# Cosine attention and a Fourier mixing layer on one core: a new order of all steps up to the first product

## The chip, the core and the metric

The kernel runs on one core of a Trainium2 chip. The metric is the device time of one execution in microseconds (us). The core's engines are TensorE (PE, with its weight loads as PEld), VectorE (DVE), ScalarE (ACT), GpSimd (POOL) and SyncE (SP); SP and POOL issue the loads, each on a DMA queue of its own.

## What is computed

Eight batches of 12 heads with 448 tokens and 64 columns. Attention works with q and k of length one; its result, 448 tokens by 768 columns, goes through a two-dimensional Fourier transform, of which the real part is added to it; then come layer normalization and a feed-forward block with 3072 hidden units and a ReLU:

```python
q_n = q / (np.linalg.norm(q, axis=-1, keepdims=True) + 1e-06)
k_n = k / (np.linalg.norm(k, axis=-1, keepdims=True) + 1e-06)
scores = np.matmul(q_n, k_n.transpose(0, 1, 3, 2)) / tau
scores = scores - np.max(scores, axis=-1, keepdims=True)
attn = np.exp(scores)
attn = attn / (np.sum(attn, axis=-1, keepdims=True) + 1e-09)
attn_out = np.matmul(attn, v)
x = attn_out.transpose(0, 2, 1, 3).reshape(B, S, H * D)
u = x + np.real(np.fft.fft(np.fft.fft(x, axis=1), axis=2))
un = (u - mean(u)) / np.sqrt(var(u) + 1e-06)
out = u + np.maximum(un @ w_ch1, 0.0) @ w_ch2
```

## The kernel before

**Stages.** The batches follow each other, and each overlaps with its neighbours: while TensorE works on the feed-forward products of batch b, the other engines prepare the heads of batch b + 1, and the attention products of b + 1 go in between. Only batch 0 has nothing ahead of it. Its start is a chain: loads of q, k and v; norms; scalings; transposes; scores; exponentials; products with v; the Fourier transform; layer normalization; and then the first product with w_ch1. The change touches this start above all.

**Names of the start, with their lines.** The twelve heads lie in six pairs, loaded in three groups: pair 0, pairs 1 and 2, pairs 3 to 5. A group has three tiles: K and Q with 384 columns for each pair (tokens 0 to 383), and a tail T with 128 columns for each pair (the last 64 tokens of q and of k). `first_norm` makes for each group:
- `ld_k`, `ld_q`, `ld_t`: the loads, on SP's queue (L1139). Before any run the planner has a list, QUEUES, with the order of the first loads of both queues; the change leaves it as it is. The v loads (L1315 to L1318), then the loads of w_ch1 (`W1_0` to `W1_11`, L1066) and of w_ch2 are on GpSimd's queue.
- `sqK`, `sqQ`, `sqT` (ACT, L1146): squares of a tile; `ssK`, `ssQ`, `ssT` (DVE, L1149): their sums for each token and head.
- `ln` (ACT, L1085), `nrm` (ACT, L1087, the root as an exponential of half the logarithm), `eps` (DVE, L1088), `rcp` (DVE, L1089): the reciprocal of norm plus epsilon.
- `scK`, `scQ` (L1172) and `scT` (L1168): the scalings of a pair, on DVE or on POOL, whichever the plan finds better.
- `tk`, `tq`, `tt` (PE, L1195 to L1220): transposes; `ek`, `eq` (L1186) and `et` (L1230, into the block-diagonal KTD) take them out of PSUM. KTD is cleared once by POOL (`ktd0`, L1009).

Then for each pair: scores `qk` (PE, L1360 and L1373), four exponentials `ex` (ACT, L1338, each over two PSUM banks of 450 columns), products with v `pv` (PE, L1391, L1397), the sums' reciprocal `rd` (L1415) and the division `x` (L1417). `fold` adds and subtracts mirrored tokens (L1434, L1441, L1468, a copy of eight columns L2101), since the transform is worked out on sums and differences. `fs` (PE, L1525) is the transform over the columns, `te` (L1547, ACT or DVE) takes it out of PSUM, `fd` (PE, L1568) is the transform over the tokens, and `u` (DVE, L1632) adds it to x with the sums for the mean. Layer normalization: `ba` (DVE, L1658, the mean), `bs` (ACT, L1662, the variance pass over 768 columns), `un` (DVE, L1674, the centred halves), `tn` (PE, L1683, transposes), `eu` (L1691, evacuations into UNT). A first product `h` is L1758: w_ch1 by UNT, first with one tile of 128 tokens (`h` of row tile 0 alone), later with a pair of row tiles (256 columns). A ReLU (L1774) follows, then the products with w_ch2 (L1902) and the output additions `fin` (POOL L1928, DVE L1939). The Fourier tables are made in the start too: sines and cosines (ACT, L1032, L1034), a negated copy of one table (`sinp` POOL L1046, `sinn` DVE L1052), halves of two rows (`half`, ACT L1049), and three loads of ScalarE's function tables (L1040, L1042, L1053). POOL makes index tables with small iotas (`ix`, L1018).

While batch 0 goes through its layer normalization, the norms of batch 1 begin in the same code (`sqK0_1`, `ssK0_1` and so on), on the same engines.

**What sets the order.** Nothing is written in the order in which it runs. Each step is an operation with its engines, its durations, a priority, the operations that it depends on (`deps`: these become semaphore waits in the program) and operations that it only has to come behind in the plan (`order`: no wait). `Plan.schedule` (L644) then simulates all engines in the builder, and at each point takes for an engine, among the operations that could start first, the one of lowest priority number. Its result is a fixed sequence for each engine. Each engine's instructions run in just that sequence, whatever the real times are. Three tables move the result: SHIFT adds a number to the priority of one operation; FLOW says how long a load takes; and LATE is a margin by which the plan puts an operation later than its load's planned landing, so that the real engine doesn't stand in front of it:

```python
            op.prio = round(op.prio + SHIFT.get(op.name, {}).get(k, 0), 4)
```

## Time and profile before

| | before |
|---|---|
| time, median of 3 runs | 575.67 us (575.16 to 577.59) |
| the profiled execution's own time | 574.34 us |
| its span in the trace | 572.5 us |
| granted TensorE clock, share of full speed | 1.0 |
| TensorE matmul busy | 552.2 us (96%), 6598 instructions |
| TensorE weight loads busy (beside the matmuls) | 432.6 us (76%) |
| VectorE busy | 439.6 us (77%), 926 instructions |
| ScalarE busy | 382.8 us (67%), 723 instructions |
| GpSimd busy | 231.5 us (40%), 338 instructions |

The rows say how long each engine worked within the span; they overlap, so they don't add up to it. The span is the traced part of the profiled execution, 1.84 us shorter than the execution's own time; that time is 1.33 us below the median of the runs. Cut into forty slices of 14.3 us each, TensorE is busy for 3 tenths of the first slice, 7 of the second, nine or more of the third and all that follow, and 8 of the last. The chain of work that ended last lies for 75% of the span on TensorE, 17% on VectorE and 5% on ScalarE.

### The profile page before, as it was taken

How to read it: one execution, taken by the hardware profiler on the slowest of the kernel's cores; microseconds unless marked ns; L12 is line 12 of the kernel's file. 1: busy time of each engine (PE TensorE's matmuls, PEld its weight loads, DVE VectorE, ACT ScalarE, POOL GpSimd, SP SyncE). 2: the span in 40 equal slices, each digit the busy share in tenths (PEclk: the TensorE clock that was granted, in tenths of full speed). 3: DMA queues.
4: the chain of work that ended last, by engine and by line, in shares of the span. 5: the costliest groups of instructions: out<-in, count | busy, mean ns of one | idle time of the engine just before them, and what ended most of it. 6: DMA issues, size and time to landing. Idle time of an engine off the chain costs nothing.

```text
span 572.5 us, 15993 instructions
## 1 busy us (share of the span) xinstructions
PE 552.2 (96%) x6598; PEld 432.6 (76%) x6598; DVE 439.6 (77%) x926; ACT 382.8 (67%) x723; POOL 231.5 (40%) x338
## 2 busy tenths in 40 slices
PE   3799999999999999999999999999999999999998
PEld 3569787686787678868778787687786886969695
DVE  8989857988488768886879668977986497987363
ACT  7898895565876676798458775696456752747171
POOL 8534424347345535453471536344532103031303
PEclk9999999999999999999999999999999999999999
DMA  9999998985349938953695549553933100023001
GB/s 193 210 239 174 170 181 123 161 180 109 113 68 114 171 87 126 138 125 92 121 125 109 83 109 132 116 128 54 142 65 34 62 1 26 32 41 73 21 36 56
DMA packets 187897, 62.19 MB, mean 109 GB/s; under 512 B 166800, under 2 KB 185616, under 8 KB 187824
## 3 DMA queue, kind: packets, MB, share of 16 engines
q1 hardware_dynamic: 129856, 38.35, 36.2%
q0 software_dynamic: 57968, 22.81, 36.0%
q8 instruction: 52, 0.85, 0.6%
q14 instruction: 21, 0.17, 0.1%
HBM read 51.90 MB, written 11.01 MB: 110 GB/s over the span
## 4 chain that ended last, share of the span: by engine, by line
PE 75%; DVE 17%; ACT 5%; issue 2%; POOL 1%; DMA 0%; DVEq 0%; POOLq 0%; ACTq 0%
PE PS L1902 26%; PE PS L1758 26%; PE PS L1853 6%; PE PS L1397 6%; PE PS L1360 5%; DVE U L1620 3%; DVE HQ L2002 2%; PE PS L1391 2%; ACT E L1338 2%; PE PS L1373 1%; DVE ACG L1609 1%; PE PS L1525 1%; DVE U L1632 1%; DVE OUTB L1939 1%; DVE SM L1272 1%
## 5 line engine op out<-in xcount | busy, mean ns | idle before, releaser
L1758 PE MATMUL PS<-UNT,W1b 128*128 128x256 bf16 (+1 forms) x1728 | 185.3, 264 | 1.2 <-ACT KTD L1230 0.4
L1758 PEld LDWEIGHTS PS<-UNT,W1b 128*128 128x128 bf16 x1728 | 154.0, 98 | 21.3 <-issue 1.7
L1338 ACT ACTIVATE E<-PS 128x900 bf16<-128x900 f32 (+1 forms) x192 | 149.3, 827 | 28.6 <-PE PS L1360 24.6
L1902 PE MATMUL PS<-W2b,HQ 128*128 128x384 bf16 x720 | 124.8, 326 | 0.0
L1283 POOL TENSOR_TENSOR QH<-STG,SM 128x256 bf16<-128x256 f32 x126 | 87.4, 720 | 90.9 <-DVE SM L1089 64.7
L1928 POOL TENSOR_TENSOR OUTB<-OUTB,U 128x192 f32<-128x192 f32 x72 | 50.8, 725 | 127.0 <-ACT OUTB L1923 125.8
L1902 PEld LDWEIGHTS PS<-W2b,HQ 128*128 128x128 bf16 x720 | 68.8, 98 | 43.3 <-issue 0.6
L1902 PE MATMUL PS<-TX,HQ 128*128 128x384 bf16 (+2 forms) x444 | 76.7, 322 | 1.6 <-DVE OUTB L1939 1.4
L1774 ACT ACTIVATE HQ<-PS 128x512 bf16<-128x512 f32 x82 | 48.8, 597 | 37.9 <-PE PS L1758 37.0
L1902 PEld LDWEIGHTS PS<-TX,HQ 128*128 128x128 bf16 x444 | 41.4, 98 | 28.2 <-DVE OUTB L1939 2.5
L2002 DVE TENSOR_TENSOR HQ<-HQ 128x1536 bf16<-128x1536 bf16 (+1 forms) x73 | 55.1, 758 | 9.1 <-ACT HQ L1774 6.3
L1272 DVE TENSOR_REDUCE SM<-QH 128x6 f32<-128x384 f32 x84 | 45.1, 544 | 13.1 <-ACT QH L1270 12.5
L1397 PE MATMUL PS<-VB,E 128*128 128x65 bf16 x1152 | 51.9, 193 | 0.0
L1270 ACT ACTIVATE QH<-STG 128x384 f32<-128x384 f32 x84 | 43.0, 521 | 10.3 <-DVE SM L1272 9.5
L1397 PEld LDWEIGHTS PS<-VB,E 128*128 128x128 bf16 x1152 | 47.9, 97 | 1.5
L1961 POOL DMA_INDIRECT out_dram<-OUTB,IDX x21 | 23.4, 1115 | 57.5 <-DVE OUTB L1939 30.1
L1774 DVE TENSOR_SCALAR HQ<-PS 128x512 bf16<-128x512 f32 x44 | 30.1, 684 | 19.7 <-PE PS L1758 19.1
L1391 PE MATMUL PS<-VZ,E 128*128 128x130 bf16 x192 | 41.6, 219 | 1.0 <-ACT E L1338 0.9
L1662 ACT ACTIVATE F<-U,MV 128x768 bf16<-128x768 bf16 x28 | 26.2, 934 | 21.2 <-DVE MV L1657 17.8
L1620 DVE SCALAR_TENSOR_TENSOR U<-ACG,X 128x768 bf16<-128x768 f32 (+4 forms) x39 | 39.3, 1014 | 0.7
L1360 PE MATMUL PS<-QK 64*128 64x225 bf16 (+2 forms) x864 | 39.1, 227 | 0.1
L1923 ACT ACTIVATE OUTB<-PS 128x384 f32<-128x384 f32 x36 | 17.6, 488 | 29.5 <-PE PS L1902 29.2
(193 smaller groups left out, 784.3 us busy)
## 6 DMA issues: line engine op xcount, KB each, us to landing
STG<-in_k_dram SPq DMA_DIRECT2D x18, 384.0 KB, 4.6
STG<-in_q_dram SPq DMA_DIRECT2D x18, 384.0 KB, 3.7
VB<-in_v_dram POOLq DMA_DIRECT2D x24, 192.0 KB, 6.7
W1b<-in_moe_w_ch_dram POOLq DMA_DIRECT2D x12, 384.0 KB, 8.0
W2b<-in_moe_w_ch_dram POOLq DMA_DIRECT2D x12, 384.0 KB, 6.7
out_dram<-OUTB SPq DMA_DIRECT2D x7, 384.0 KB, 4.4
W2b<-in_q_dram SPq DMA_DIRECT2D x2, 576.0 KB, 10.1
W2b<-in_k_dram SPq DMA_DIRECT2D x2, 576.0 KB, 11.0
```

What stands on the lines that cost most here:

```text
L1272: P.add("dve", lambda v, o=SS[:, i, H // ns * x:H // ns * (x + 1)], sq=sq: v.tensor_reduce(o, sq.rearrange("p (h d) -> p h d", d=DH), AX.X ...
L1283: r = v.tensor_tensor(v3(qh)[:, h:h + 4], v3(buf)[:, h:h + 4], RN[:, i, h:h + 4].unsqueeze(2).to_broadcast((128, 4, DH)), AluOp.mult)
L1338: return a.activation(o, self.PS[:, bk:bk + nc_, 0:SQ2], ACTF.Exp, scale=1.0 / self.tau)
L1360: i = pe.matmul(self.PS[:, bk + h, c0:c0 + n], self.KT[r, jj, kt * 128:(kt + 1) * 128], self.QT[r, jj, cols], start=True, stop=True)
L1391: r = pe.matmul(o, st(6), self.VZ[:, j, :], start=not split, stop=(split and i == 0), skip_group_check=True)
L1397: r = pe.matmul(o[:, 65 * h:65 * h + 65], st(2 * kt + h), self.VB[:, kt, 2 * j + h, :], start=(split and i == h == kt == 0), stop=((not sp ...
L1620: self.snu.append(P.add("dve", lambda v: v.scalar_tensor_tensor(two(U[o0:o0 + n, ut, :]), src, 1.0, two(X[i0:i0 + n, x, :]), AluOp.mult, A ...
L1758: r = pe.matmul(self.PS[:, bk, x * n:(x + 1) * n], self.W1b[:, j, ft * 128:(ft + 1) * 128], self.UNT[:, j, cs], start=(j == 0), stop=(j == ...
L1774: return e.activation(o, i, ACTF.Relu) if e is self.nc.scalar else e.tensor_relu(o, i)
L1902: r = pe.matmul(self.PS[:, bk, 0:n], lhs(f), rhs(f), start=(start and f == 0), stop=(stop and f == NF // 2 - 1), skip_group_check=True)
L1928: r = g.tensor_tensor(self.OUTB[:, ob, xs], self.OUTB[:, ob, xs], self.U[:, ut, xs], AluOp.add)
L2002: P.add("dve", lambda v: v.tensor_tensor(cs(o), cs(a), cs(bq), op), 0.16 + 0.3 * len(ks), -0.5, f"{nm}{ks[0]}_{b}", reads=rd, writes=[x fo ...
```

## The change

Five things are changed; the instructions themselves stay what they were, but for the engine that some of them run on.

1. **The table SHIFT is replaced as a whole**, up to the last batch. So the sequence of every engine is another one, in the start and behind it.
2. **Margins.** LATE gets six entries for the start: for the squares of the second group's K (0.85) and T (0.95), of the third group's Q (1.25), T (2.6) and K (2.3), and for the first product with v (2.6). In the plan these now come that much behind the planned landings.
3. **The clearing of KTD** (`ktd0`) gets a real dependency on the first scalings of pair 0, K, Q and T. So it waits for VectorE in the program, where it waited for nothing of that kind.
4. **The scalings of pair 0** can run on VectorE only; the plan had put one on GpSimd.
5. **Orders for the plan** (no waits): GpSimd's small iotas (`ix`) and the clearing of pads come behind the last v load of batch 0; the transform's second half `fd` of batch 0 is chained; the squares of K and T of batch 1 come behind ScalarE's `te`; their sums come behind the first two `eu`; the variance pass `bs` of the first row tile comes behind its `eu`; the residual additions from the third on behind its `un`; the copies `cd1` to `cd5` (the mirrored half of a table) behind its `eu`; and the last function table load behind `te`.

```diff
 SHIFT = {
...
-    "scK0_0": {0: 40.2716}, "scQ0_0": {0: 379.426}, "scT0_0": {0: 381.7288}, "et0_0": {0: 8.4556}, "ld_k1_0": {0: 119.799},
...
-LATE = {r"sq6_[2-7]": 4.0, r"W[12]_\d+": 1.5, "tmd": 2.0, r"sq\d_\d": 2.0, r"sq[KQT]\d_1": 1.5, ...
+LATE = {r"sqK1_0": 0.85, r"sqT1_0": 0.95, r"sqQ2_0": 1.25, r"sqT2_0": 2.6, r"sqK2_0": 2.3, r"pv00_0": 2.6, r"sq6_[2-7]": 4.0, ...
...
-        P.add("pool", lambda g: g.memset(self.KTD[:], 0.0), 0.8, -3, "ktd0", after=[tas],
+        self.ktd0 = P.add("pool", lambda g: g.memset(self.KTD[:], 0.0), 0.8, -3, "ktd0", after=[tas],
...
                 P.add("act", lambda e, sq=sq, buf=buf: e.activation(sq, buf, ACTF.Square), t_act(w), pg[g], f"sq{nm}{g}_{b}",
-                      reads=names, writes=sqn[g][i], order=[self.exps[-1]] if b else [])
+                      reads=names, writes=sqn[g][i], order=[self.exps[-1]] + self.te[1:] * (i != 1) if b else [])
...
-                                 t_dve(w), pg[g], f"ss{nm}{g}_{b}", reads=sqn[g][i], writes=[f"SS_{a + j}{i}" for j in range(n)], order=sc if b else []))
+                                 t_dve(w), pg[g], f"ss{nm}{g}_{b}", reads=sqn[g][i], writes=[f"SS_{a + j}{i}" for j in range(n)], order=sc + self.un0 * (i != 1) if b else []))
...
-                    sc.append(P.add("dve" if b else ("dve", "pool"), fn, ...
+                    sc.append(P.add(("dve", "pool") if b == 0 and g else "dve", fn, ...
                                     writes=qhn[g][i] if j == 0 else [qhn[g][i][-1] + f"_{j}"],
                                     after=[sc0[i]] if j else []))
                     if j == 0:
                         sc0.append(sc[-1])
+                        if (b, g) == (0, 0):
+                            self.ktd0.deps.add(sc[-1])
...
             self.vl.append(op)
+            if b == 0 and t == 3:
+                for x in P.ops:
+                    if re.fullmatch(r"ix\d+|pads", x.name):
+                        x.order = tuple(x.order) + (op,)
...
-            P.add(es, ev, [t_act(n_) if e == "act" else t_dve(n_) for e in es], pj, f"te{blk}_{b}",
+            te = P.add(es, ev, [t_act(n_) if e == "act" else t_dve(n_) for e in es], pj, f"te{blk}_{b}",
...
+            if es == ("act",):
+                self.te.append(te)
...
-                                         tiles=(tile,), acquire=tile if sg or b else None, margin=0.2))
+                                         tiles=(tile,), acquire=tile if sg or b else None, margin=0.2, order=self.fd_ops[-1:] if b == 0 else ()))
...
-            P.add("act", lambda a, ut=ut, ns_=ns_, mean=mean, var=var: a.activation(
+            bs = P.add("act", lambda a, ut=ut, ns_=ns_, mean=mean, var=var: a.activation(
...
+                if late:
+                    bs.order = tuple(bs.order) + tuple(P.ops[-2:])
+                    self.un0 = P.ops[-2:]
+                    for u in [x for x in self.snu[2:] if x.name == "u0_0"] + [x for x in self.snu if x.name == "u1_0"]:
+                        u.order = tuple(u.order) + (un,)
+                    for x in P.ops:
+                        if x.name in ("cd1", "cd2", "cd3", "cd4", "cd5"):
+                            x.order = tuple(x.order) + tuple(self.un0)
+                    self.ldt.order = tuple(self.ldt.order) + tuple(self.te)
```

The three places below show the sequence of one engine each. Line numbers are those of the two kernels apart: in the changed kernel the same line stands some 55 higher (L1146 is now L1201, L1172 is L1227, L1066 is L1121).

ScalarE near its start, before: squares (into HQ and W2b), the two halved rows (CS, 1x225), a table load, the logarithm (L1085) and root (L1087) of pair 0's norms, the squares of the second group's T, K and Q, the first evacuation (into QK).

```order
L1146 ACTIVATE HQ<-TX 128x384
L1049 ACTIVATE CS<-CS 1x225
L1146 ACTIVATE HQ<-TX 128x128
L1049 ACTIVATE CS<-CS 1x225
L1040 ACT_TABLE_LOAD
L1085 ACTIVATE SM<-SM,MV 128x14
L1087 ACTIVATE SM<-SM 128x14
L1146 ACTIVATE HQ<-TX 128x256
L1146 ACTIVATE W2b<-TX 128x768
L1146 ACTIVATE HQ<-TX 128x1152
L1186 ACTIVATE QK<-PS 128x384
```

The same place after:

```order
L1201 ACTIVATE HQ<-TX 128x128
L1201 ACTIVATE HQ<-TX 128x384
L1095 ACT_TABLE_LOAD
L1140 ACTIVATE SM<-SM,MV 128x14
L1104 ACTIVATE CS<-CS 1x225
L1142 ACTIVATE SM<-SM 128x14
L1104 ACTIVATE CS<-CS 1x225
L1201 ACTIVATE HQ<-TX 128x1152
L1201 ACTIVATE HQ<-TX 128x256
L1201 ACTIVATE W2b<-TX 128x768
L1243 ACTIVATE QK<-PS 128x384
```

The two halved rows come behind the logarithm, one of them between it and the root, and the wide square of Q (128x1152) comes ahead of the squares of T and K.

GpSimd behind its v loads and index tables, before: loads of w_ch1 with scalings of T (TX) and of K and Q (QH) among them.

```order
L1066 DMA W1b<-in_moe_w_ch_dram 128x6x256 x2
L1168 TENSOR_TENSOR TX<-TX,SM 128x128
L1066 DMA W1b<-in_moe_w_ch_dram 128x6x256
L1172 TENSOR_TENSOR QH<-TX,SM 128x384
L1066 DMA W1b<-in_moe_w_ch_dram 128x6x256
L1168 TENSOR_TENSOR TX<-TX,SM 128x128
L1172 TENSOR_TENSOR QH<-TX,SM 128x384
L1066 DMA W1b<-in_moe_w_ch_dram 128x6x256
L1172 TENSOR_TENSOR QH<-TX,SM 128x384
L1066 DMA W1b<-in_moe_w_ch_dram 128x6x256 x4
```

The same place after:

```order
L1064 MEMSET KTD 128x768
L1121 DMA W1b<-in_moe_w_ch_dram 128x6x256 x3
L1223 TENSOR_TENSOR TX<-TX,SM 128x128
L1121 DMA W1b<-in_moe_w_ch_dram 128x6x256
L1223 TENSOR_TENSOR TX<-TX,SM 128x128 x2
L1227 TENSOR_TENSOR QH<-TX,SM 128x384
L1121 DMA W1b<-in_moe_w_ch_dram 128x6x256
L1227 TENSOR_TENSOR QH<-TX,SM 128x384
L1121 DMA W1b<-in_moe_w_ch_dram 128x6x256 x7
```

The clearing of KTD stands just ahead of the loads of w_ch1 now; before, it came right behind the v loads, some ten index rows earlier. Three scalings of T follow with one weight load among them, and two scalings of K or Q in place of three.

VectorE around the evacuation of the column transform (CAST E), before: the subtractions of `fold` (L1468), a sum of squares of batch 1 (SM out of W2b, L1149), the evacuation (L1547), another sum, the residual additions (L1632), the mean (L1658), the centred halves (L1674), the first evacuation into UNT (L1691).

```order
L1468 TENSOR_TENSOR ACG<-F 128x2x2x64
L1468 TENSOR_TENSOR ACG<-F 128x4x64
L1149 TENSOR_REDUCE SM<-W2b 128x3x6
L1547 CAST E<-PS 65x450
L1149 TENSOR_REDUCE SM<-OUTB 128x3x6
L1045 TENSOR_SCALAR MV<-TX 128x1
L1632 SCALAR_TENSOR_TENSOR U,ACG<-PS,X 128x384 x2
L1658 TENSOR_SCALAR MV<-ACG 128x1
L1632 SCALAR_TENSOR_TENSOR U,ACG<-PS,X 128x384
L1674 TENSOR_SCALAR F<-U,MV 128x384 x2
L1632 SCALAR_TENSOR_TENSOR U,MV<-PS,X 64x384
L1691 CAST UNT<-PS 128x3x128
```

The same place after:

```order
L1529 TENSOR_TENSOR ACG<-F 128x4x64
L1529 TENSOR_TENSOR ACG<-F 128x2x2x64
L1100 TENSOR_SCALAR MV<-TX 128x1
L1101 TENSOR_SCALAR CS<-TX 128x2x385
L1608 CAST E<-PS 65x450
L1204 TENSOR_REDUCE SM<-W2b 128x3x6
L1695 SCALAR_TENSOR_TENSOR U,ACG<-PS,X 128x384 x2
L1721 TENSOR_SCALAR MV<-ACG 128x1
L1737 TENSOR_SCALAR F<-U,MV 128x384 x2
L1695 SCALAR_TENSOR_TENSOR U,ACG<-PS,X 97x384
L1695 SCALAR_TENSOR_TENSOR U,ACG<-PS,X 128x384
L2173 COPY CS<-CS 97x2x96
```

The evacuation (CAST E, L1608) has gone ahead of both sums of batch 1; the negated table (CS out of TX, L1101) came from GpSimd and stands ahead of it; and the centred halves (L1737) follow the mean without a residual addition between.

Some moves in other places, read from the same listings: before, four of the index iotas stood between the clearing of VZ and the v loads, and all of them come behind the v loads now. An evacuation of a transposed q goes ahead of ScalarE's square of the last K. Logarithm and root of the third group come one exponential earlier. A copy of eight columns in the second `fold` goes from VectorE to ScalarE, as do two of VectorE's evacuations into UNT of the later row tiles. Between the first residual addition and the last evacuation into UNT VectorE has one sum of squares, one large and one small scaling of batch 1 more. In batch 5 the output additions (`fin`, POOL) of one pair of row tiles now have two whole scalings, six instructions, between the first and the others.

## Rows read from the trace of the kernel before

**Rows 1.** Windows: stretch, us, busy us of the engines, PEclk, DMA share, GB/s.

```profile
48.50:63.50 15.00, 13.89 (x212) 12.16 (x213) 13.94 (x40) 13.79 (x32) 8.41 (x11) 1.00 1.42 171
63.50:120.00 56.50, 56.50 (x602) 43.01 (x601) 44.42 (x99) 40.20 (x80) 19.74 (x28) 1.00 1.32 157
300.00:400.00 100.00, 99.02 (x1233) 77.81 (x1232) 78.30 (x166) 73.42 (x144) 44.08 (x59) 1.00 0.73 106
```

**Rows 2.** Timeline of TensorE, 0 to 80 us: start, us, instruction, [idle before, releaser].

```profile
41.48 0.98 PE L1525 MATMUL PS<-CS,ACG 128*65 128x225 bf16 x8
...
48.46 6.90 PE L1758 MATMUL PS<-UNT,W1b 128*128 128x128 bf16 x120 [0.22 <-ACT UNT L1691]
...
62.21 0.82 PE L1758 MATMUL PS<-UNT,W1b 128*128 128x256 bf16 x6 [0.41 <-ACT KTD L1230]
```

**Rows 3.** Timeline of ScalarE, 0 to 66 us.

```profile
7.79 0.39 ACT L1049 ACTIVATE CS<-CS 1x225 bf16<-1x225 bf16 x1
...
11.16 0.84 ACT L1146 ACTIVATE W2b<-TX 128x768 f32<-128x768 f32 x1 [0.81 <-DMA TX<-in_k_dram]
11.91 1.15 ACT L1146 ACTIVATE HQ<-TX 128x1152 f32<-128x1152 f32 x1
...
14.93 2.94 ACT L1338 ACTIVATE E<-PS 128x900 bf16<-128x900 f32 x4
...
18.17 1.16 ACT L1146 ACTIVATE W2b<-TX 128x1152 f32<-128x1152 f32 x1
...
28.44 8.99 ACT L1338 ACTIVATE E<-PS 128x900 bf16<-128x900 f32 x12 [0.27 <-PE PS L1360]
...
47.02 0.92 ACT L1662 ACTIVATE F<-U,MV 128x768 bf16<-128x768 bf16 x1
```

**Rows 4.** Timeline of VectorE, 0 to 66 us.

```profile
8.52 0.38 DVE L1052 TENSOR_SCALAR HQ<-CS 128x900 bf16<-128x900 bf16 x1
...
10.08 0.71 DVE L1088 TENSOR_SCALAR SM<-SM 128x14 f32<-128x14 f32 x1 [0.31 <-ACT SM L1087]
...
11.27 1.14 DVE L1172 TENSOR_TENSOR QH<-TX,SM 128x384 bf16<-128x384 f32 x1
...
15.39 1.50 DVE L1172 TENSOR_TENSOR QH<-TX,SM 128x384 bf16<-128x384 f32 x3
...
23.33 0.42 DVE L1089 RECIPROCAL SM<-SM 128x42 f32<-128x42 f32 x1
...
24.07 1.22 DVE L1172 TENSOR_TENSOR QH<-TX,SM 128x384 bf16<-128x384 f32 x2
...
41.34 1.34 DVE L1149 TENSOR_REDUCE SM<-W2b 128x18 f32<-128x1152 f32 x1
...
58.51 1.02 DVE L1691 CAST UNT<-PS 128x384 bf16<-128x384 f32 x2
```

**Rows 5.** Timeline of GpSimd, 0 to 66 us.

```profile
5.36 3.28 POOL L1315 DMA_DIRECT2D VB<-in_v_dram  x3 [0.37 <-POOL IDX L1018]
...
10.02 0.74 POOL L1009 MEMSET KTD<- 128x768 bf16 x1
...
24.30 0.57 POOL L1168 TENSOR_TENSOR TX<-TX,SM 128x128 bf16<-128x128 f32 x1 [1.42 <-DVE TX L1168]
25.04 0.94 POOL L1172 TENSOR_TENSOR QH<-TX,SM 128x384 bf16<-128x384 f32 x1 [0.17 <-POOL TX L1168]
26.52 0.88 POOL L1066 DMA_DIRECT2D W1b<-in_moe_w_ch_dram  x1 [0.55 <-DVE RD L1415]
```

**Rows 6.** Timeline of SyncE's queue, 0 to 66 us: issue of loads.

```profile
6.90 1.68 SPq L1139 DMA_DIRECT2D TX<-in_k_dram  x2
```

**Rows 7.** DMA issues: tile, KB each, median us from issue to landing.

```profile
TX<-in_k_dram SPq DMA_DIRECT2D x1, 576.0 KB, 9.9
```

**Rows 8.** Timeline of all engines, 182 to 199 us.

```profile
182.83 3.75 POOL L1283 TENSOR_TENSOR QH<-STG,SM 128x256 bf16<-128x256 f32 x4
...
190.44 2.12 PE L1902 MATMUL PS<-TX,HQ 128*128 128x384 bf16 x12 [1.01 <-DVE OUTB L1939]
```

13 lines of the change are left out of this document (7 added, 6 removed), and 933 rows, old and new, of the table SHIFT.

## The prediction

> **What bounds the kernel now.** I read the windows by stage first. From 63.5 us on TensorE is busy 56.50 of 56.50 us, and still 99.02 of 100 us in 300 to 400 [rows 1]: some 509 us in which the order of the other engines costs next to nothing. What can be won is the time until TensorE gets there. Its timeline gives two marks: the first product starts at 48.46, the first product of a pair of row tiles at 62.21 [rows 2]; between them VectorE is busy 13.94 of 15.00 us and ScalarE 13.79 [rows 1], so both are near their limit there. Ahead of 48.46 the timelines of ScalarE and VectorE [rows 3, 4] show a chain that changes hands: norms of the first heads, exponentials from 14.93, squares and norms of the last three head pairs (18.17 to 23.75), twelve exponentials from 28.44 to 37.43 without a pause, then fold and Fourier products. So I follow five marks through the new order: first exponential E (14.93), end of the third group's reciprocal R (23.33 + 0.42 = 23.75), end of the last exponential T (28.44 + 8.99 = 37.43), first product (48.46), first pair product (62.21).
>
> **A. To E.** VectorE's add of epsilon to 14 columns took 0.71 us beside GpSimd's clearing of KTD (10.02, 0.74 [rows 5]), while 900 columns took 0.38 at 8.52: at least 0.33 of it is waiting. The first scaling took 1.14 beside one on GpSimd, where three undisturbed ones took 1.50, 0.50 each [rows 4]. The clearing now stands behind the first scalings, and both large scalings are VectorE's: minus 0.33 to 0.7 and minus 0.64, plus 0.50 for the second scaling, plus 0.38 for the negated table, which slips in between. On ScalarE the halvings (7.79, 0.39, and its like before it [rows 3]) leave the place ahead of the logarithm's table load, and one comes in between logarithm and root: 0.3 to 0.4 won. Together the first scaled heads are ready between 0.4 and 0.9 earlier. But they don't set E: ScalarE's square at 11.16 waits 0.81 for a load of k. What stands behind it is the path: 11.16 to 14.93 is 3.77, of it 1.05 (11.91 up to the next instruction, 1.15 with its tail) the wide square of q, which now runs ahead, in that wait. So E could be 13.9. Against it: four index rows leave the place ahead of GpSimd's v loads, and 5.36 [rows 5] becomes about 4.3, so v shares the DMA engines with k for a microsecond more. Bounds for the delay of k: 0, and the whole 1.0; I take 0.4, a bit under half, as two queues then share. E = 14.3, 0.65 earlier.
>
> **B. E to R.** From E to the square of the last k passed 18.17 - 14.93 = 3.24; the new order puts an evacuation of q ahead of it too, 0.5 by the pair at 58.51 [rows 4]: 14.3 + 3.75 = 18.05. The load (issued at about 7.7, the second of the two at 6.90 [rows 6], 9.9 to its landing [rows 7]) lands at 17.6, with the same 0.4 at 18.0. So this square wins 0.1 only, and nothing if k comes a little later. The win is behind it: 18.17 to 23.75 was 5.58, and logarithm and root now come one exponential earlier, 2.94 / 4 = 0.74. R = 18.05 + 5.58 - 0.74 = 22.9, **0.85 earlier** (0.3 if the load is later by the whole 1.0).
>
> **C. R to the fourth head pair.** 23.75 to 28.44 was 4.69. Now GpSimd has three tail scalings with a weight load among them: 0.57, then a gap of 0.55 and the issue of 0.88, 0.57, a gap of 0.17, 0.57 = 3.3 [rows 5] (from 24.30 on). Behind the last of them stand transposes and two score products. Before, the like passage from the end of a scaling (25.04 + 0.94) to 28.44 took 2.46, with evacuations in it; TensorE alone needs less, and I take 1.4, between 1 and 2.46. 4.7, so nothing won, nothing lost; bounds 4.3 and 5.8. The third pair's exponentials don't fill this time any more: their score products stand behind the same transposes, so they wait in it.
>
> On the port: the two scalings at 24.07 took 1.22, so 0.11 each over 0.50 [rows 4], beside GpSimd's at 24.30. The Trainium skill (SBUF — State Buffer, section "SBUF: two separate sides") says that a VectorE instruction with two SBUF inputs and a GpSimd one that reads SBUF lock each other out for the whole instruction. The row at 11.27 bears that out, the row at 24.07 hardly. By the rule alone VectorE would lose two of GpSimd's scalings more in C, 1.1; by the row at 24.07, 0.2.
>
> **D. The twelve exponentials.** 8.99 before. One score product now stands behind a scaling of GpSimd's that stands behind another weight load; a wait of 0 to 0.9 (one issue). The old 8.99 has some slack itself, 12 x 0.74 = 8.9, so I leave it. T = 36.6, **0.85 earlier**.
>
> **E. T to the first product.** 11.03 before. VectorE's evacuation ahead of the Fourier products stood behind a sum of squares of the next batch (41.34 + 1.34 = 42.68 [rows 4]); now it goes ahead, and ScalarE's half ahead of a square. It can't win more than the distance to the end of its own products, 41.48 + 0.98 = 42.46 [rows 2], if the sum alone had held it: 0.2; with ScalarE's half, which stood behind a whole square of 1.05, up to 0.9. I take 0.45. The copy of eight columns that moves to ScalarE may take 0.2 of it back (it is in the 0.45). The sign copy moves from GpSimd to VectorE, 0.4 by the row of 900 columns, while VectorE waits for TensorE: nothing, or 0.4 if that cover fails. Behind the Fourier products the evacuation into UNT stood behind the variance pass (47.02, 0.92 [rows 3]), and a residual addition ahead of the centred halves; both now come later. 0 to 0.92; I take 0.45, as the halves of the same chain are waited for anyway. **0.9 earlier**: first product at 46.7, 1.75 earlier.
>
> **F. First product to first pair.** 13.75 before. From the first residual addition to the last UNT evacuation (58.51 + 1.02 [rows 4]) VectorE gets a sum of squares (1.34), a large scaling (0.5) and a small one (half that) more and two evacuations (1.02) less; a ReLU and a table copy come, a residual addition and two table operations go, taken as even: 1.1 later. Behind that point 2.7 passed until the pair (59.53 to 62.21), since two scalings, a sum and tail evacuations came last; now the scalings stand ahead, and the pair hangs on ScalarE's last evacuations: 1.2, so 1.5 won. But ScalarE has two variance passes of 0.92 in a row and two of VectorE's evacuations. Between 0.4 won and 0.9 lost I take **0.2 lost**. The W1 loads should keep up: GpSimd starts them earlier.
>
> **G. The rest.** The same instructions in a newly searched order. TensorE is full there [rows 1]; I count nothing, plus or minus 1.5 for waits that move.
>
> **Sum.** 0.85 + 0.9 - 0.2 = 1.55. The profiled execution took 574.34, so its like would take 572.8; the median of the three runs, 575.67, lies 1.3 above it, and against it the forecast is **574.1**, 0.3% less.
>
> **Rivals.** *All of it arrives.* The v loads don't disturb k: E = 13.9, the last square of k at 17.65, R = 22.5, 1.25 earlier; C at its lower bound 0.4, E 0.9, F 0.4: 2.95, so 572.7. For it: the 0.71 and 1.14 on VectorE are plain loss. Against: the square at 11.16 waits for a load that nothing makes earlier.
> *Nothing arrives.* VectorE and ScalarE are full between the marks [rows 1], and what was won ahead of 48.46 is waited for again ahead of the pair, by evacuations on ScalarE or by the last W1 loads: 0.3 left, 575.4.
> *Slower: GpSimd's output additions queue behind scalings.* In batch 5 the new order puts two whole scalings (six instructions) between the first and the other additions of a pair, which followed each other before. A like place of the old kernel shows the price: four such instructions, 3.75 us, end at 186.58, the additions come after them, and TensorE stands 1.01 at 190.44 [rows 8]. If these scalings wait for their own norms, nothing of the 3.75 is hidden: 574.1 + 3.75 = 577.9. From an exposed wait of 1.55 on it decides the sign. For it: TensorE's queue is in order. Against: such places in batches 2 and 3 are gone in the new order.
>
> **How the numbers follow.** Forecast (gain 0.5 to 2.7) 0.45, all of it 0.30, nothing 0.12, slower 0.13. 0.5% is 2.9 us, about what a measurement of this kernel tells from no change. Faster than 572.8: most of the second case and a little of the first, 0.32. Slower than 578.5: part of the last case, with more than one such wait, 0.12. Within: 0.56. The range goes from 571.5 (the second case, and 1.2 less of waits in the rest) to 577.2 (into the slower case).
>
> **What would show it.** Right: first exponential near 14.3, R near 22.9, exponentials ending near 36.6, first product near 46.7, first pair near 60.65, TensorE full after. A is wrong if that square of k starts after 11.9, or the epsilon add still takes 0.7; B if the last square of k starts after 18.6; C if the fourth pair's exponentials start over 5.3 behind R; E if the evacuation still waits for a sum; F if first product and first pair are over 14.5 apart; G if TensorE waits in the rest show new pauses of over 1.5 in all.

## The result, and the profile after

The changed kernel takes 577.56 us (median of 18 runs, 576.42 to 579.85), the kernel before 575.48 in the same measurement: ratio 1.0042, with a 95% interval of 1.0032 to 1.0052. (Each ratio is worked out from the single runs and isn't the quotient of the two medians, which is 1.0036 here; differences in us are those of the medians.) So it is 2.1 us slower, 3.5 above the forecast of 574.1 and 0.4 beyond the end of its range. On another chip it took 577.07 against 575.07 (1.0033, 1.0021 to 1.0045). The profiled execution took 578.65, its span is 576.7; those of before were 574.34 and 572.5. This pair is 4.2 apart, twice the distance of the medians, so one trace of each isn't enough here, and a second trace of the changed kernel (own time 576.64) stands beside the first in what follows. In the changed kernel's rows L1146 is L1201, L1172 is L1227, L1338 is L1399, L1758 is L1830, L1902 is L1974.

The five marks (us). E is the first exponential, R the end of the third group's reciprocal, T the end of the last exponential:

| | v loads go out | square of K, group 2, starts | E | R | T | first product | first pair |
|---|---|---|---|---|---|---|---|
| before | 5.36 | 11.16 | 14.93 | 23.75 | 37.43 | 48.46 | 62.21 |
| predicted | about 4.3 | about 11.6 | 14.3 | 22.9 | 36.6 | 46.7 | 60.65 |
| after | 4.64 | 13.18 | 15.89 | 24.01 | 38.17 | 48.27 | 62.78 |
| after, second trace | 4.52 | 12.64 | 15.35 | 23.47 | 37.63 | 47.73 | 61.61 |

The rows of after for the start, in the order SP's loads of k as the DMA view has them (KB, us to landing), GpSimd's v loads, ScalarE's two squares of K and the first exponentials, VectorE's epsilon and first scalings, TensorE's transposes of the fourth pair, first product and first pair (timelines: start, us, instruction, [idle before, releaser]):

```profile
TX<-in_k_dram SPq DMA_DIRECT2D x1, 576.0 KB, 11.3
TX<-in_k_dram SPq DMA_DIRECT2D x1, 384.0 KB, 7.5
```

```profile
4.64 3.28 POOL L1372 DMA_DIRECT2D VB<-in_v_dram  x3 [0.91 <-DMA TX<-in_q_dram]
```

```profile
13.18 0.84 ACT L1201 ACTIVATE W2b<-TX 128x768 f32<-128x768 f32 x1 [1.30 <-DMA TX<-in_k_dram]
...
15.89 1.73 ACT L1399 ACTIVATE E<-PS 128x900 bf16<-128x900 f32 x2
...
19.57 1.19 ACT L1201 ACTIVATE W2b<-TX 128x1152 f32<-128x1152 f32 x1
```

```profile
10.04 0.17 DVE L1143 TENSOR_SCALAR SM<-SM 128x14 f32<-128x14 f32 x1
...
10.94 1.01 DVE L1227 TENSOR_TENSOR QH<-TX,SM 128x384 bf16<-128x384 f32 x2
```

```profile
27.23 0.50 PE L1264 MATMUL PS<-TX,QH 128*128 128x128 bf16 x3 [0.48 <-POOL TX L1223]
...
48.27 7.70 PE L1830 MATMUL PS<-UNT,W1b 128*128 128x128 bf16 x132 [0.41 <-ACT UNT L1754]
...
62.78 2.79 PE L1830 MATMUL PS<-UNT,W1b 128*128 128x256 bf16 x24
```

VectorE's part of the start went as foreseen: epsilon 0.17 instead of 0.71, two scalings of 0.5 each instead of one of 1.14 [rows 4]. But ScalarE stands 1.30 before the square of K, where it stood 0.81 and two us earlier [rows 3]: this load, the one of 384 KB, took 7.5 us to land, and in before 5.5:

```profile
TX<-in_k_dram SPq DMA_DIRECT2D x1, 384.0 KB, 5.5
```

Less was moved in this time by all loads together. From 8 to 10 us it was 221 GB/s in before (first row) and 133 in after (second row; the last column, the others as in [rows 1]):

```profile
8.00:10.00 2.00, 2.00 (x21) 1.94 (x19) 1.77 (x4) 1.94 (x5) 1.98 (x3) 1.00 1.24 221
```

```profile
8.00:10.00 2.00, 1.69 (x17) 1.69 (x18) 2.00 (x5) 1.57 (x5) 1.79 (x7) 1.00 1.28 133
```

The last k load took 11.3 instead of 9.9 [rows 7].

Behind the first pair, the windows of before (first fence; the stretches 63.5 to 120 and 300 to 400 are in [rows 1]), of after, and of the second trace of after (columns as in [rows 1]):

```profile
120.00:300.00 180.00, 178.20 (x2053) 139.02 (x2052) 139.74 (x290) 123.58 (x235) 89.14 (x120) 1.00 0.79 120
...
400.00:560.00 160.00, 159.58 (x1936) 126.97 (x1931) 116.55 (x227) 89.41 (x167) 38.82 (x58) 1.00 0.25 48
```

```profile
63.50:120.00 56.50, 54.86 (x587) 40.94 (x585) 46.23 (x103) 38.41 (x74) 19.60 (x26) 1.00 1.08 157
120.00:300.00 180.00, 176.61 (x2029) 136.80 (x2028) 139.72 (x288) 122.12 (x235) 83.92 (x115) 1.00 0.78 118
300.00:400.00 100.00, 100.00 (x1205) 79.58 (x1203) 77.95 (x164) 73.96 (x145) 43.74 (x60) 1.00 0.61 107
400.00:560.00 160.00, 159.46 (x1974) 126.34 (x1972) 114.69 (x227) 93.00 (x172) 42.90 (x63) 1.00 0.26 51
```

```profile
63.50:120.00 56.50, 54.86 (x587) 40.91 (x585) 46.73 (x102) 38.36 (x75) 20.64 (x28) 1.00 1.07 154
120.00:300.00 180.00, 177.38 (x2043) 137.63 (x2041) 139.63 (x286) 121.19 (x233) 84.42 (x117) 1.00 0.77 118
```

TensorE's idle time in these four stretches is 0 + 1.80 + 0.98 + 0.42 = 3.2 us before, and 1.64 + 3.39 + 0 + 0.54 = 5.6 after (4.8 in the second trace, where the last two stretches have 0 and 0.55). Counted over all that lies behind the first pair, TensorE alone (before, after, the second trace of after):

```profile
62.21:571.00 508.79, 504.65 (x5895) 1.00 0.66 97
```

```profile
62.78:575.00 512.22, 505.93 (x5897) 1.00 0.60 97
```

```profile
61.61:573.00 511.39, 505.94 (x5897) 393.63 (x5895) 385.86 (x791) 330.89 (x629) 194.47 (x271) 1.00 0.60 97
```

TensorE's last product ends at 570.06 before, 574.28 after and 572.36 in the second trace, so the three stretches hold 507.85, 511.50 and 510.75 us of which the busy time leaves 3.2, 5.57 and 4.81 idle. The distance of the traces from before, 4.2 and 2.3, is now whole: 0.57 and -0.60 in the start, 2.4 and 1.6 more idle time, and 1.3 in both by which TensorE is busy longer with the same products (two more are tiny ones, of 64 columns). Each group of products has the same count and nearly the same mean in both kernels (the 384-column ones 326 ns, the 256-column ones 273), so the 1.3 lies in how they follow each other, spread too thin for any row to show. It belongs to the order and not to one trace: behind the first pair TensorE is busy for 505.7 to 506.0 us in the nine traces with the new order there (these two and seven of the runs below), for 504.6 to 504.8 in four of the five with the old order throughout, and for 505.3 in the fifth, which has more filler products in its start. What makes it stays open.

The idle time sits at few places. Here are the two largest of after: batch 1's Fourier products with VectorE's subtractions ahead of them and GpSimd's scaling of batch 2 beside them, and output products near 297 us.

```profile
100.54 0.60 PE L1586 MATMUL PS<-CS,F 128*97 128x225 bf16 x4 [1.19 <-DVE F L1546]
...
103.42 0.20 PE L1638 MATMUL PS<-CS,E 97*128 97x96 bf16 x1 [0.45 <-ACT E L1607]
```

```profile
97.25 1.81 DVE L1529 TENSOR_TENSOR ACG<-F 128x764 bf16<-128x764 bf16 x2
...
99.44 1.04 DVE L1546 TENSOR_TENSOR F<-ACG 128x388 bf16<-128x388 bf16 x2
```

```profile
97.97 2.29 POOL L1340 TENSOR_TENSOR QH<-STG,SM 128x256 bf16<-128x256 f32 x3
```

```profile
296.98 0.82 PE L1974 MATMUL PS<-TX,HQ 128*128 128x384 bf16 x4 [1.47 <-DVE OUTB L2011]
```

The expectations below count a wait from one product's start to the next, less the product's own columns. So 1.36 there is the 1.19 of the row, and 1.64 the 1.47.

### The profile page after: what moved, and what is told of

It is laid out like the page before. It is cut to its first block, busy times and chain, and to the rows that moved or that the text cites. A ratio compares the mean times of both kernels' runs of the same rounds, so it can differ in the third digit from the quotient of the medians.

```text
span 576.7 us, 15979 instructions
## 1 busy us (share of the span) xinstructions
PE 553.7 (96%) x6592; PEld 432.6 (75%) x6592; DVE 441.8 (77%) x927; ACT 383.7 (67%) x724; POOL 227.4 (39%) x336
## 4 chain that ended last, share of the span: by engine, by line
PE 56%; DVE 7%; ACT 2%; issue 1%; DVEq 0%; ACTq 0%
PE PS L1830 20%; PE PS L1974 20%; PE PS L1925 6%; PE PS L1458 4%; PE PS L1421 3%; DVE HQ L2074 2%; PE PS L1452 1%; DVE U L1683 1%; PE PS L1434 1%; DVE OUTB L2011 1%; PE PS L1582 1%; ACT E L1399 1%; DVE ACG L1672 1%; DVE HQ L1945 0%; PE PS L1641 0%
## 5 line engine op out<-in xcount | busy, mean ns | idle before, releaser
L1830 PE MATMUL PS<-UNT,W1b 128*128 128x256 bf16 (+1 forms) x1728 | 185.1, 264 | 1.0 <-DVE MV L1720 0.5
L1399 ACT ACTIVATE E<-PS 128x900 bf16<-128x900 f32 (+1 forms) x192 | 149.4, 825 | 30.5 <-PE PS L1421 23.2
L1830 PEld LDWEIGHTS PS<-UNT,W1b 128*128 128x128 bf16 x1728 | 153.8, 98 | 21.1 <-issue 1.7
L1974 PE MATMUL PS<-W2b,HQ 128*128 128x384 bf16 x720 | 125.1, 326 | 0.0
L1974 PEld LDWEIGHTS PS<-W2b,HQ 128*128 128x128 bf16 x720 | 68.9, 98 | 42.6 <-issue 0.6
L2000 POOL TENSOR_TENSOR OUTB<-OUTB,U 128x192 f32<-128x192 f32 x72 | 49.1, 703 | 118.0 <-ACT OUTB L1995 116.1
L1974 PE MATMUL PS<-TX,HQ 128*128 128x384 bf16 (+2 forms) x444 | 76.9, 322 | 1.9 <-DVE OUTB L2011 1.7
L1974 PEld LDWEIGHTS PS<-TX,HQ 128*128 128x128 bf16 x444 | 41.2, 98 | 30.1 <-DVE OUTB L2011 3.3
L1372 POOL DMA_DIRECT2D VB<-in_v_dram x24 | 25.4, 1069 | 30.0 <-PE PS L1458 25.5
```

The source lines that it names most:

```text
L1399: return a.activation(o, self.PS[:, bk:bk + nc_, 0:SQ2], ACTF.Exp, scale=1.0 / self.tau)
L1830: r = pe.matmul(self.PS[:, bk, x * n:(x + 1) * n], self.W1b[:, j, ft * 128:(ft + 1) * 128], self.UNT[:, j, cs], start=(j == 0), stop=(j == ...
L1974: r = pe.matmul(self.PS[:, bk, 0:n], lhs(f), rhs(f), start=(start and f == 0), stop=(stop and f == NF // 2 - 1), skip_group_check=True)
L2000: r = g.tensor_tensor(self.OUTB[:, ob, xs], self.OUTB[:, ob, xs], self.U[:, ut, xs], AluOp.add)
```

## The experiments

Two theories: the loss has **two places** (the start, and new waits behind the pair), and in the start it comes from the **loads** alone. Where a run keeps rows "word for word", each engine's sequence was written out and taken as it stands; everything else is planned as in its kernel.

**Which part loses.** The sequences of both kernels were joined at the first pair.

```diff
-for op in ready[e]:
+for op in [x for x in ready[e] if key[x] == ROWS[e][len(self.order[e])]]:
```

> The changed kernel's rows on every engine up to the first product of a pair of row tiles (62.78 us in its trace, 62.21 in the one before), and from there on the old kernel's rows, word for word. Theory 'two places': the start loses 0.6 and the rest loses about 1.5 of the 2.1 us between the medians; then this kernel comes 0.6 above the kernel before, 576.1, first pair near 62.8, and TensorE's waits behind it add up to about 6 us as in the trace of before, with no wait over 1 at batch 1's Fourier products (near 100 us). Rival 'start alone': the waits behind the pair differ by chance from execution to execution, and the start costs it all: 577.5. Rival 'rest alone': 575.5.

Measured: 576.52 against 575.84 (1.0015, 1.0004 to 1.0026), first pair at 61.94, and no idle row at the Fourier products near 100. It has one wait of its own, where the sequences are joined:

```profile
66.98 2.14 PE L1830 MATMUL PS<-UNT,W1b 128*128 128x256 bf16 x18 [1.01 <-DVE HQ L1846]
```

> The mirror of it: the old kernel's rows up to the first pair, then the changed kernel's rows. Theory 'two places': first pair at 62.2, 1.5 us above the kernel before, 577.0, with the wait of about 1.4 ahead of batch 1's Fourier products and the one of about 1.6 near 297 us again. Rival 'start alone': 575.5 and neither wait. Rival 'rest alone': 577.5.

Measured: 577.67 against 575.84 (1.0042, 1.0027 to 1.0057), first pair at 61.69, and both waits of the changed kernel came along:

```profile
99.37 0.60 PE L1525 MATMUL PS<-CS,F 128*97 128x225 bf16 x4 [1.19 <-DVE F L1485]
...
295.03 0.82 PE L1902 MATMUL PS<-TX,HQ 128*128 128x384 bf16 x4 [1.26 <-DVE OUTB L1939]
```

So the larger part of the loss is the rest (1.8 us by the medians of this run). The start loses 0.7 in the first run, but 1.01 of its trace is the wait at the splice; so the new start by itself wins 0.3 at most by these medians, far from 1.55. "Start alone" falls: with the old start the loss stays. The two parts don't add up exactly (0.7 and 1.8 against 2.1 by the medians; by the ratios 0.9 and 2.4 against 2.4).

**What delays k.** Six iotas back ahead of the v loads, in two ways. The first run moves them in GpSimd's sequence before the plan is made, so that the fillers are planned anew; the second moves them behind the plan, and this is its edit:

```diff
+L = self.P.order["pool"]
+i = [op.name for op in L].index("ld_v2_0")
+xs = [op for op in L if op.name in ("ix6", "ix7", "ix0", "ix8", "ix1", "ix9")]
+L[:] = L[:i] + xs + [op for op in L[i:] if op not in xs]
```

> The changed kernel with six of GpSimd's index iotas put back ahead of the v loads, which so are issued at about 5.3 us in place of 4.64; everything else as in the changed kernel. Theory 'loads': the k load of the second group landed 2.0 us later (13.16 against 11.14) because the v loads went out 0.7 earlier; here it lands near 11.3, ScalarE's square of it starts near 11.9 (after: 13.18), the first exponential near 14.3 (after: 15.89), the reciprocal of the third group ends near 23.2 (24.01), and the time is 0.5 to 0.9 less than the changed kernel's, 576.8. Rival 'order': the square of q that now runs ahead of it and the evacuations behind it set the first exponential; the k load lands near 13 as before or the exponential stays at 15.5 or later, and the time stays 577.5.

Measured: 579.52 against 575.84 (1.0074, 1.0059 to 1.0090): slower, though the v loads went out at 5.99, the square of K started at 11.40 without a wait, E was 14.95 and R 22.90. T was 38.01 all the same. The plan had put 18 filler products in front of the fourth pair's transposes:

```profile
26.20 1.18 PE L2228 MATMUL PS<-TX 128*128 128x128 bf16 x18 [0.17 <-DVE QK L1243]
27.22 0.49 PE L1264 MATMUL PS<-TX,QH 128*128 128x128 bf16 x3
```

The same move behind the plan, with the fillers as they were:

> As the run with six iotas ahead, but TensorE's filler products stay where the changed kernel has them (there 18 more of them, 1.18 us, stood ahead of the transposes of the fourth pair and ended at 27.2 us). Theory 'loads': the k load of the second group lands near 11.3, first exponential near 14.9, third reciprocal near 22.9, and now the last exponential ends 0.8 to 1.1 earlier than in the changed kernel (38.17), near 37.2, first product near 47.4, first pair near 61.8; time 0.7 to 1.0 less than the changed kernel's. Rival 'GpSimd queue': the transposes wait for GpSimd's scalings all the same, the last exponential ends at 37.9 or later and nothing is won.

Measured: 576.23 against 575.07 (1.0023, 1.0013 to 1.0032); the changed kernel itself on the same chip took 577.07:

> The changed kernel itself, on the chip of these runs, to compare them with: 577.6, marks within 0.3 us of its first trace, and the waits near 100 (1.36) and 297 us (1.64) again.

So 0.84 is won by moving six iotas of 0.2 us. The rows of that run on ScalarE and TensorE:

```profile
11.39 0.83 ACT L1201 ACTIVATE W2b<-TX 128x768 f32<-128x768 f32 x1
14.57 1.73 ACT L1399 ACTIVATE E<-PS 128x900 bf16<-128x900 f32 x2
...
29.44 7.29 ACT L1399 ACTIVATE E<-PS 128x900 bf16<-128x900 f32 x10 [0.44 <-PE PS L1421]
```

```profile
46.83 7.73 PE L1830 MATMUL PS<-UNT,W1b 128*128 128x128 bf16 x132 [0.41 <-ACT UNT L1754]
...
60.86 2.79 PE L1830 MATMUL PS<-UNT,W1b 128*128 128x256 bf16 x24
```

E 14.57, R 22.58, T 36.73, first product 46.83, first pair 60.86: in this trace all five lie within 0.4 us of the predicted marks. It is an early one of its kind. In the four other traces with the new start, this load in time and the fillers from 7.5 us, E was 14.95 to 15.55 and the first pair came at 61.47 to 62.34. The old kernel with that one part of the change:

> The old kernel with this one part of the change alone: its four iotas ahead of the v loads go behind them, so that these are issued at about 4.7 in place of 5.36. Theory 'loads': the k load of the second group lands near 13.1 (before: 11.14), and since in this order the square of k stands ahead of the wide square of q, all of it arrives: the first exponential at 16.5 to 16.9 (before: 14.93), the first product 0.5 to 1.5 later (before: 48.46), time 576.0 to 577.0. Rival 'order': k lands as before, exponential at 14.9, time 575.5.

Measured: 578.72 against 575.84 (1.0054, 1.0033 to 1.0074). v at 4.54, and the square of K waits 2.38 us:

```profile
13.10 0.84 ACT L1146 ACTIVATE W2b<-TX 128x768 f32<-128x768 f32 x1 [2.38 <-DMA TX<-in_k_dram]
...
16.93 2.98 ACT L1338 ACTIVATE E<-PS 128x900 bf16<-128x900 f32 x4 [0.17 <-PE PS L1360]
```

First product 50.06, first pair 63.87. The marks are those of the theory; the time is 1.2 more than they explain. Its trace has one new wait near the end, of 1.66 where before has 0.17, which would cover that (518.12, first products waiting for UNT); why it came isn't known. With all iotas ahead, v went out at 7.93:

> The changed kernel with all of GpSimd's index iotas and the clearing of pads ahead of the v loads, which so go out near 7.3 us (before: 5.36, after: 4.64). Theory 'loads': the delay of k grows with the head start of v; the k load of the second group lands near 10.0 to 10.5, the first exponential is near 14.2 and the marks up to the last exponential are 0.3 to 0.6 ahead of the run with six iotas, as long as v itself (then landing near 21 to 22) isn't waited for; time as that run or 0.3 less. Rival 'v': the first products with v wait for their load, and the last exponential ends 0.5 to 1.5 later than in the run with six iotas (36.73).

Measured: 577.83 against 575.43 (1.0041, 1.0027 to 1.0055), square of K at 11.39 as with six, E 15.20, first pair 61.61. So the delay doesn't grow evenly with the head start. It looks like a step. Of the 17 traces of this case, six have v out at 4.52 to 4.64: this load took 6.9 to 7.9 us to land, and the square of K started at 12.55 to 13.57. Eleven have v out at 5.35 to 7.93: the load took 5.5 to 6.1, and the square started at 11.16 to 11.76. No run lies between 4.64 and 5.35. Nor is it a matter of sharing alone, as from 8 to 10 us all loads together moved 131 to 174 GB/s in the six and 219 to 262 in the eleven; why, stays open. The later E of this run is told in the last section.

**What happens behind the pair.** GpSimd's scaling held back until the Fourier products are done:

```diff
+named = {op.name: op for op in self.P.ops}
+named["sc0_2"].deps.add(named["fs1_1"])
```

> The changed kernel with one wait more: GpSimd's first scaling of batch 2 (three instructions, 97.97 to 100.26 us, beside VectorE's subtractions of batch 1's fold) waits until the Fourier products that need this fold are done. Theory 'port': the two subtractions take 1.02 us as in the kernel before (after: 1.81) and the two last ones 0.63 (after: 1.04); TensorE's wait ahead of the Fourier products falls from 1.36 to about 0.2, and the time by about 1.2. Rival 'cover': the wait comes from eight W2 products (1.3 us) that ran ahead of the Fourier products in the kernel before and run behind them now, with VectorE's work as long as before; then the wait stays at 1.0 or more and the time stays.

Measured: 579.44 against 575.07 (1.0084, 1.0063 to 1.0105). The subtractions do as the port theory says, the time doesn't. VectorE:

```profile
97.12 1.03 DVE L1529 TENSOR_TENSOR ACG<-F 128x764 bf16<-128x764 bf16 x2
...
98.53 0.63 DVE L1546 TENSOR_TENSOR F<-ACG 128x388 bf16<-128x388 bf16 x2
...
104.57 2.33 DVE L1683 SCALAR_TENSOR_TENSOR U<-ACG,X 128x768 bf16<-128x768 f32 x1
```

Without the scaling beside them the subtractions take 1.03 and 0.63 instead of 1.81 and 1.04, and the Fourier products at 99.41 have no idle time before them. But the first residual addition took 2.33, beside GpSimd's next scalings (six, 4.92 us from 104.87). That they lie side by side isn't enough to explain it: in the changed kernel the same six lie there too (4.90 us from 104.77), and this addition took 0.96:

```profile
105.81 0.96 DVE L1683 SCALAR_TENSOR_TENSOR U<-ACG,X 128x768 bf16<-128x768 f32 x1
```

The rows differ in the order of the starts: there the addition began 1.04 behind the first scaling, here 0.3 ahead of it. The next addition took 1.11 in both. TensorE waits for what hangs on them:

```profile
120.33 4.86 PE L1830 MATMUL PS<-UNT,W1b 128*128 128x256 bf16 x43 [1.32 <-DMA UNT<-F]
```

The wait was moved, not removed: 1.19 went and 1.32 came. The rest of the loss isn't explained: behind the first pair this trace has 511.36 us, only 0.6 more than the second trace of the changed kernel, and the medians differ by 2.4.

In its sign this agrees with the rule of the Trainium skill that the prediction weighed (SBUF — State Buffer, section "SBUF: two separate sides"). Its price isn't that of whole instructions throughout: beside three scalings of 0.6 to 0.8 us VectorE lost 0.8 and 0.4 in two pairs of subtractions, and beside the six 1.4 in an addition that took 0.96 beside them in the changed kernel.

The copy near 297 us, back on ScalarE:

```diff
+x = [op for op in D if op.name == "ktd5"][0]
+D.remove(x)
+x.eng = "act"
+C.insert([op.name for op in C].index("fm0_3") + 1, x)
```

> The changed kernel with one copy into KTD of batch 5 (0.73 us on VectorE at 292.05) back on ScalarE, where the kernel before had it (0.52, ScalarE idle there). Theory: VectorE's queue is what the output additions near 297 wait in; TensorE's wait there falls from 1.64 to about 0.9 and the time by about 0.7. Rival: the additions wait for GpSimd's clear-up of the pair, and nothing moves.

Measured: 576.58 against 575.07 (1.0021, 1.0010 to 1.0031), 0.5 less than the changed kernel on this chip, which the spread of the runs doesn't tell from nothing. The wait itself is halved, as the theory has it:

```profile
295.95 0.82 PE L1974 MATMUL PS<-TX,HQ 128*128 128x384 bf16 x4 [0.69 <-DVE OUTB L2011]
```

All at once, with the old order at batch 1's fold (the sequences of three engines there as before the change):

> The changed kernel with six iotas ahead of the v loads, and with the old kernel's order at two places of the rest: at batch 1's fold (norm of batch 2's first head ahead of the last division, GpSimd's first scaling ahead of the v loads of batch 2, one W2 product of four more ahead of the Fourier products and four ahead of the second ones) and the copy into KTD of batch 5 on ScalarE. Theory: the wait near 98.6 (1.34 and 0.61) falls below 0.5 in all and nothing comes back at 120 us, the one near 294 from 1.63 to 0.9; time 2.0 to 2.7 below the run with six iotas (576.2 where before was 575.1), 573.6 to 574.2, 1 below the kernel before. Rival 'given back': the six scalings behind slow VectorE's additions, a wait over 1 comes near 120, and the time is 575 or more.

Measured: 578.57 against 575.58 (1.0067, 1.0048 to 1.0086). The rival was right, and worse than it said:

```profile
102.49 2.12 PE L1974 MATMUL PS<-W2b,HQ 128*128 128x384 bf16 x12 [1.38 <-DVE OUTB L2010]
...
121.32 3.87 PE L1830 MATMUL PS<-UNT,W1b 128*128 128x256 bf16 x34 [1.95 <-DVE F L1737]
```

The order at batch 1's fold is good only with the order around it: a piece of the old sequence in the new one costs 3.3 us at two places that had no wait, twice what it takes away near 100 us (1.19 and 0.45).

**Where the 0.9 us between T and the first product come from.** The old kernel with both evacuations ahead of batch 1's sum and square:

```diff
+for e, x, y in (("dve", "ssQ0_1", "te1_0"), ("act", "sqK0_1", "te1_0")):
+    op = [o for o in self.P.order[e] if o.name == x][0]
...
+    L.insert([o.name for o in L].index(y) + 1, op)
```

> The old kernel with one part alone: VectorE's evacuation of the column transform ahead of its sum of squares of batch 1, and ScalarE's ahead of its square. Theory: what the change wins between the last exponential and the first product (11.03 before, 10.10 after) comes from this; it becomes 10.2 to 10.6, the first product comes near 47.8, the first pair 0.4 to 0.8 earlier, time 0.4 to 0.8 less than before. Rival 1: it comes from the order behind the Fourier products (variance pass behind the evacuations into UNT); then under 0.3 is won. Rival 2: the sums that now come later are waited for ahead of the first pair, which stays at 62.2.

Measured: 578.27 against 575.43 (1.0053, 1.0040 to 1.0067), but this says nothing on the question. The fillers ahead of the Fourier products wait for the moved sum, and the products stand behind them:

```profile
45.28 1.18 PE L2156 MATMUL PS<-TX 128*128 128x128 bf16 x18 [1.98 <-DVE SM L1149]
```

With fillers that don't wait for it:

> The old kernel with both evacuations of the column transform ahead of batch 1's sum and square, and fillers that wait for the fold instead of the moved sum. Theory: last exponential to first product becomes 10.2 to 10.6 (before 11.03, after 10.10), the first pair comes 0.4 to 0.8 earlier, time 0.4 to 0.8 less than before. Rival 1: the gain comes from behind the Fourier products; under 0.3 is won. Rival 2: the first pair stays at 62.2, and the time too.

Measured: 576.05 against 575.58 (1.0009, 1.0000 to 1.0017). T to first product took 11.45 (38.21 to 49.66), not less than 11.03. With both of them moved to stand behind it, the evacuation wins nothing. The two sums (1.34 each) now stand together behind it, and the first residual addition starts at 46.41, 8.2 behind T, where it stood 7.3 behind T before and 7.0 after. By these rows, what the change wins is that only one sum is left there, and that the centred halves follow the mean at once: 46.58 in after, 8.4 behind T, 9.2 before. No run tries either of them alone.

**A better version?** The changed start with six iotas ahead, and from 63 us of the plan on the old sequences:

> The changed kernel's rows up to 63 us of the plan, with six iotas ahead of the v loads (fillers as planned), and from there on the old kernel's rows. Theory 'two places, and the start only lost by the v loads': first pair near 60.9 as in the run with six iotas and the same fillers, behind it the waits of the kernel before (no 1.35 near 99 us, none over 0.9 near 295), so the time is 1.0 to 1.5 below the kernel before, 574.0 where before is 575.2. Rival 'given back': waits of the rest take up what the start wins (the first pair's evacuations, or W1 and v loads), and the time is that of before.

Measured: 575.34 against 575.43 (0.9998, 0.9988 to 1.0009): level with the kernel before. First pair 61.47; so by these traces the start gives 0.74. Behind it the row is

```profile
61.47:571.00 509.53, 505.23 (x5897) 394.10 (x5895) 381.63 (x790) 329.20 (x630) 196.74 (x271) 1.00 0.65 97
```

and TensorE's last product ends at 570.07, where before ends it at 570.06: 508.60 us, 3.37 idle (0.17 more) and 505.23 busy (0.58 more). The win of the start is given back behind it, most of it in the busy time that no row explains. More fillers, from 5 us on, in the old kernel and in this mix:

```diff
-self.P.fill(7.5, first, self.id_op, warm(self.ID))
+self.P.fill(5.0, first, self.id_op, warm(self.ID))
```

> The old kernel with 18 filler products more on TensorE, from about 5 us on in place of 7.5; nothing else. Theory 'pace': TensorE is at its fast pace by 12.5 us in every execution (three transposes take 0.35 to 0.5, not 0.85), the first exponential comes at 14.9 or up to 0.3 before, never at 16.2, and the median is 0.3 to 0.8 below the kernel before's. Rival: the pace is not what moves it, or the fillers hold something up; time as before or 0.3 more.

> The changed kernel's start with six iotas ahead and the old kernel's rest, with 24 filler products more from about 5 us on. Theory 'pace': first exponential at 14.0 to 14.5 (15.01 in the run without them), first pair at 60.3 to 60.9, time 0.5 to 1.2 below the kernel before. Rival: first pair at 61.5 and the time that of before.

Measured: 576.54 against 575.56 (1.0014, 1.0005 to 1.0023) and 575.63 against the same (1.0012, 1.0000 to 1.0025). E was 15.88 and 14.37, the first pair at 62.93 and 60.78. The second of them wins 1.43 in the start against before's trace and gives it back behind the pair, 509.55 us against 507.85. No version beats the kernel before.

## Why the prediction was wrong

**The forecast summed 0.85 + 0.9 - 0.2 = 1.55 won, nothing from the rest. Two terms of it failed: the delay of k in the start, and the rest, which was put at nothing.**

**A, wrong: the delay of k.** It was taken as 0.4 with bounds of 0 and 1.0, "a bit under half, as two queues then share". It was 1.5 to 2.0 (square of K at 12.64 and 13.18, not 11.16 + 0.4), and 1.4 to 2.4 in all six traces with v that early (counted from 11.16). A microsecond of head start was taken as the most that it can cost. The runs show something like a step that costs more than the head start, with fewer bytes moved by all loads together, where the prediction had two queues share what is moved. Everything else in A came (0.17, 0.50, the square of q ahead), and with the head start undone E was 14.57 in one trace and 14.95 to 15.55 in four, still later than 14.3. In the second trace of after the terms miss by 1.05 (A), -0.5 (B), -0.2 (C), 0.6 (D), nothing (E) and -0.1 (F), so the first pair's 0.96 is A's; in the first trace A misses by 1.6 and F by 0.6. The prediction named the place and the sign ("A is wrong if that square of k starts after 11.9") and missed the size.

**B, right in the mechanism, 0.5 too high.** E to the last square of K took 3.68 (predicted 3.75), E to R 8.12 (8.6); the win of the earlier logarithm is there. That square started at 19.57 and 19.03, behind the 18.6 that B named as its own sign, but through A's delay.

**C right, D 0.6 too low.** R to T took 14.15 to 14.16 in the two traces of after and with six iotas ahead, 13.68 before. C is right: the transposes of the fourth pair wait for GpSimd's tail scaling (27.23, 0.48 idle) as feared, and the twelve exponentials start 4.54 behind R (28.55; 4.7 predicted). They take 9.62 instead of 8.99, and 0.44 of it is a wait for score products, which stand behind products with v on TensorE (29.41 to 30.46); whether a scaling of GpSimd's holds them up further back, no run tells:

```profile
30.87 1.53 ACT L1399 ACTIVATE E<-PS 128x900 bf16<-128x900 f32 x2 [0.44 <-PE PS L1421]
```

That the first pair didn't come later still is luck: B's error and D's cancel.

**E, right in sum, wrong in where.** T to first product took 10.10 (10.1 predicted). Half of the 0.9 won was put on the evacuation. In the run above that gave nothing; by the rows the residual additions and centred halves gave it, which no run tests by itself.

**F, right in two of three runs.** 13.88 and 14.03 (13.95 predicted), 14.51 in the first trace, just over the 14.5 that F named as its own sign; there the means of two row tiles came together at 54.89.

**G, wrong: the rest.** It was counted at nothing, "plus or minus 1.5". It costs 1.8 by the medians of the run with the old start; in the two traces 2.9 and 3.7, of which 1.6 and 2.4 are idle time and 1.3 is a longer busy time. The reason given, that TensorE is full there [rows 1], tells that the old order was good there, and nothing of a new one. The sign could have been foreseen in part: a sequence in which TensorE hardly waits has little to win by a move and more to lose. The slower rival looked at the right kind of thing (GpSimd's scalings in the way) at the wrong place: batch 5's additions cost nothing (idle 0.54 from 400 to 560 us, 0.42 before). The scalings beside VectorE's fold in batch 1, and VectorE's copy near 297 us, were the largest places. The waits that the change takes away (the stretch 300 to 400 us has none now, 0.98 before) are smaller.

## What to carry to other kernels

Where the first engine is already full, as TensorE was here behind the first pair, price a new order at a loss, not at nothing: this one cost 2.9 and 3.7 us there. Look in the new order for each place at which GpSimd's operations with data come to lie beside VectorE's on the path. A load that is let go earlier is a cost to the loads that the path waits for, and here its price was like a step, not like a share: six index rows put back ahead of it won 0.8 us. A sequence that was searched as a whole is hard to mend piece by piece. The six index rows paid, the copy's 0.5 lies within the spread of the runs, and the held back scaling and the old order of the fold cost time.

## What the runs showed of the hardware that was not expected

**TensorE's pace in the start differs between executions of like rows.** Three transposes of q in the kernel before, and the same three in the run with the evacuation first, in which nothing ahead of 40 us was changed:

```profile
12.97 0.49 PE L1207 MATMUL PS<-TX,QH 128*128 128x128 bf16 x3
```

```profile
13.45 0.85 PE L1207 MATMUL PS<-TX,QH 128*128 128x128 bf16 x3
```

The granted clock is 1.00 in both windows, the level of 2.4 GHz, but the second goes at little more than half the rate. E was 14.93 in the one and 16.24 in the other, with the square of K at 11.16 and 11.21. The rows of TensorE ahead of it are alike in both, so what decides it stays open. The four traces with the old start rows fall in two pairs, E at 14.83 and 14.93 and at 16.20 and 16.24: the trace of before that the prediction was worked out from is one of the early ones, and the 1.3 between them is as large as what the start was to win. So a single trace of a start is to be compared with that in mind. With fillers from 5 us the transposes took 0.50 in the mix (E 14.37).

In the old kernel the fillers from 5 us didn't help, and there the granted clock does show it. TensorE stood 1.77 us ahead of 11.83, and from 12 to 15 us the clock was 0.50, the level of 1.2 GHz (us, busy us, granted clock, DMA share, GB/s); the transposes of q took 0.85 there:

```profile
12.00:13.00 1.00, 1.00 (x11) 0.50 1.93 160
```

**Fillers are rows like others.** Products that only keep TensorE busy held up real ones twice, by 1.0 us (27.22 instead of about 26) and by 2 us through the wait that they carry.
